# Softmax, prologue and weight conversion of a fused attention and MoE kernel rewritten: one exponential per row group, loads in another order, low words written into the sum's buffer

## The chip, the core and the metric

The kernel runs on one core of a Trainium2 chip. The core has five engines with a queue of instructions each, taken in order: TensorE (PE; its weight loads are shown apart as PEld), VectorE (DVE), ScalarE (ACT), GpSimd (POOL) and SyncE (SP, which issues most of the transfers here). Sixteen DMA engines move data between HBM and the on-chip buffer. The metric is the device time of one execution in microseconds, the median of several.

## The reference

Three stages, one after the other, on 4608 tokens of 512 features:

```python
# attention inside chunks of 64 tokens, 8 batches x 8 heads x 576 x 64
scores = scale * (q_c @ k_c.transpose(...))          # scale = 1/sqrt(64)
scores = scores - scores.max(-1)
attn = exp(scores); attn = attn / (attn.sum(-1) + 1e-9)
x = attn @ v_c                                        # -> (4608, 512)
# a dense layer pair, 512 -> 2048 -> 512
h = x @ w_in
x = (h * sigmoid(1.702 * h)) @ w_out
# routed layer pair: 8 experts, one per token, 512 -> 1024 -> 512
do = (x @ w_skip) > 0; e = argmax(x @ w_gate); p = softmax(x @ w_gate)[e]
out[do] = x + p * (relu(x @ w1[e]) @ w2[e]); out[~do] = x
```

The weights `w_in` and `w_out` come as 64-bit floating-point numbers.

## The kernel before, in words

Each matrix product of the dense and the routed layers is made of three in a 32-bit matmul type: an operand is split into a high half (a cast by ScalarE) and a low half (the rest, by VectorE), and high x high, high x low and low x high are summed. The dense layers run in nine blocks of 512 tokens. In a block TensorE goes over 16 slices of 128 of the inner dimension: `emit_h` (12 matmuls of 512 columns, L296) fills `hps`, then `sg` (tanh on ScalarE, L299; a product on VectorE, L300), `gh` (ScalarE, L306) and `gl` (VectorE, L307) follow, and `emit_y` (12 matmuls, L316, L317, L320) adds to `yps`. The y of a slice is written one slice behind its h. After the blocks the routed layers run.

**Attention.** The four tiles of 128 tokens that block 0 needs are worked in a prologue (`A[0]` to `A[3]`); the other 32 (`St`) are worked inside blocks 0 to 7, five in block 0 and four in each later one, at slices given by a table, two tiles' matmuls at a time (`burst`). A tile has these steps: loads of q, k and v; `a`, transposes of q and k by TensorE and copies by ScalarE; `b`, scores, the row maximum (L166) and the subtraction of it (L168) by VectorE, the exponential by ScalarE (L173); `c0`, sum, addition, reciprocal and product by VectorE (L176 to L179); `c1`, transposes; `d`, the product with v and its copies to `x1` (L212). `split_x1` makes the high and low halves `xh` (L285, ScalarE) and `xl` (L286, VectorE) of the block's activations.

**Conversion of the weights.** `w_in` and `w_out` are 32 halves of 128x512 numbers of 64 bits, 512 KB each (`Half`; half 2i is `w_in`'s slice i, half 2i+1 is `w_out`'s). `load` brings one into one of three `raw` buffers. `s0`, two ScalarE steps: `r`, the high words with the exponent moved (L255, "the r-step" below), and `lf`, the low words scaled (L256), into a single buffer. `s1`: VectorE shifts `r` (L262, the shift) and joins the sign (L263, the or-step) into `a`, which has two buffers; POOL adds `lf` (L264). `s3`: ScalarE casts `a` to `whi` (L276), VectorE takes the rest as `wlo` (L277). A `tick` does one such step for several halves in turn and issues the load of the half three further on. Slice i of block 0 needs halves 2i and 2i+1; in all later blocks the converted weights stay.

**What sets the order.** The text calls `tick` once per step of the prologue from its second step on, and twice per slice of block 0. The text's order is not the engines' order: the program is built with a scheduler that reorders each engine's queue by its own times. What counts is therefore the built order. Buffers that two uses share tie them: the three `raw` buffers (a load waits until the half three before has been read by ScalarE and VectorE), the four `x2` buffers for `r`, and PSUM's two banks with the tag `at` for the scores.

## Time and profile before

| | us |
|---|---|
| median of 3 runs | 1224.9 (1224.62 to 1226.09) |
| the profiled execution, its own time | 1227.84 |
| its span, first to last instruction | 1226.1 |
| TensorE busy | 1182.7 (96%) |
| TensorE weight loads busy | 991.8 (81%) |
| VectorE busy | 783.9 (64%) |
| ScalarE busy | 490.2 (40%) |
| POOL busy | 144.6 (12%) |
| first `xh` / first `xl` / first matmul of block 0 | 47.25 / 48.34 / 48.73 |
| first store of block 0's result | 166.58 |
| the same store of blocks 1, 2 and 3 | 265.93, 364.98, 464.02 |

Times are counted from the start of the span. A row of a list of groups gives the line of the kernel, the engine, the operation, output and inputs, the shape, the count, then busy time and the mean of one, then the idle time of the engine just before these instructions and what ended it. A row of the timeline gives start, duration, engine, line and operation, and in brackets the idle time just before with its releaser. Matmuls overlap each other, so their durations add up to more than the time they take.

### The profile page before, as it was taken

The numbers are of one execution on the slowest core, as the hardware profiler recorded it, in microseconds if no ns is written. First come the engines' busy times: TensorE is split into PE (matmuls) and PEld (weight loads), VectorE is DVE, ScalarE is ACT, GpSimd is POOL, SyncE is SP. The second block draws the span as 40 slices with busy tenths as digits, with TensorE's granted clock in tenths as the row PEclk, the third lists the DMA queues.
The fourth block names the chain that finished last, engine by engine and source line by source line (L and its number), as shares of the span: only waits on it lengthen the run. The fifth ranks groups of instructions, "written<-read, shape, count | busy, mean of one in ns | idle before, by whom it ended". The sixth has DMA issues, their size and how long they took to land. (4 is left out here: it accounts for less than half of the span.)

```text
span 1226.1 us, 20893 instructions
## 1 busy us (share of the span) xinstructions
PE 1182.7 (96%) x7984; PEld 991.8 (81%) x7984; DVE 783.9 (64%) x1771; ACT 490.2 (40%) x825; POOL 144.6 (12%) x137
## 2 busy tenths in 40 slices
PE   6798999999999999999999999999999999999995
PEld 4576788888888888888888888888788989999885
DVE  5889578369349548647736935943985686665531
ACT  5867443343332333324334333332344454444320
POOL 2344000010010010000001001001021023231110
PEclk9999999999999999999999999999999999999998
DMA  9756331131122113113113113202344677666540
GB/s 211 208 175 178 112 102 27 44 104 26 27 68 78 28 31 107 32 31 95 35 36 104 26 28 92 55 10 69 130 139 131 215 170 265 215 228 227 195 144 8
DMA packets 181848, 129.00 MB, mean 105 GB/s; under 512 B 122336, under 2 KB 155360, under 8 KB 181617
## 3 DMA queue, kind: packets, MB, share of 16 engines
q1 hardware_dynamic: 177072, 117.09, 33.4%
q0 software_dynamic: 4672, 10.54, 2.5%
q8 instruction: 64, 1.05, 0.4%
q14 instruction: 40, 0.32, 0.1%
HBM read 103.59 MB, written 25.04 MB: 105 GB/s over the span
## 5 line engine op out<-in xcount | busy, mean ns | idle before, releaser
L316 PE MATMUL yps<-whi,gh 128*128 128x512 f32 x576 | 228.7, 397 | 6.4 <-ACT gh L306 6.4
L296 PE MATMUL hps<-xh,whi 128*128 128x512 f32 x576 | 231.6, 405 | 3.2 <-DVE sg L300 3.2
L296 PE MATMUL hps<-xl,whi 128*128 128x512 f32 x576 | 227.5, 395 | 0.0
L296 PE MATMUL hps<-xh,wlo 128*128 128x512 f32 x576 | 227.0, 394 | 0.0
L317 PE MATMUL yps<-wlo,gh 128*128 128x512 f32 x576 | 225.6, 392 | 0.0
L300 DVE SCALAR_TENSOR_TENSOR sg<-sg,hps 128x512 f32<-128x512 f32 x144 | 98.3, 684 | 172.1 <-ACT sg L299 171.1
L353 DVE CUSTOM_DVE_ANT_0 junk<-x,wg 128x512 f32<-128x512 f32 x256 | 175.8, 687 | 4.0
L543 DVE TENSOR_TENSOR elo<-rawe,ehi 128x1024 fp32r<-128x1024 f32 x88 | 107.6, 1224 | 84.6 <-ACT ehi L542 84.5
L320 PE MATMUL yps<-whi,gl 128*128 128x512 f32 x576 | 156.0, 393 | 0.0
L299 ACT ACTIVATE sg<-hps 128x512 f32<-128x512 f32 x144 | 85.8, 598 | 163.4 <-PE hps L296 163.2
L542 ACT CAST ehi<-rawe 128x1024 fp32r<-128x1024 f32 x88 | 92.3, 1049 | 139.6 <-PE h2p L608 69.4
L306 ACT ACTIVATE gh<-sg 128x512 fp32r<-128x512 f32 x144 | 91.0, 632 | 118.3 <-DVE sg L300 104.8
L316 PEld LDWEIGHTS yps<-whi,gh 128*128 128x128 f32 x576 | 108.3, 188 | 30.9 <-ACT gh L306 7.8
L296 PEld LDWEIGHTS hps<-xh,whi 128*128 128x128 f32 x576 | 108.5, 190 | 26.3 <-DVE sg L300 4.1
L296 PEld LDWEIGHTS hps<-xh,wlo 128*128 128x128 f32 x576 | 108.9, 189 | 22.6
L320 PEld LDWEIGHTS yps<-whi,gl 128*128 128x128 f32 x576 | 108.0, 189 | 22.6 <-DVE gl L307 0.3
L317 PEld LDWEIGHTS yps<-wlo,gh 128*128 128x128 f32 x576 | 108.5, 188 | 21.8
L296 PEld LDWEIGHTS hps<-xl,whi 128*128 128x128 f32 x576 | 109.2, 190 | 20.6
L307 DVE SCALAR_TENSOR_TENSOR gl<-sg,gh 128x512 fp32r<-128x512 f32 x144 | 99.0, 688 | 33.4 <-ACT gh L306 21.7
L406 POOL DMA_INDIRECT tab<-pr,pos x36 | 37.8, 1049 | 682.3 <-DVE st L166 335.0
L608 PE MATMUL h2p<-xT,ehi 128*128 128x256 f32 x640 | 117.2, 283 | 0.0
L608 PEld LDWEIGHTS h2p<-xT,ehi 128*128 128x128 f32 x640 | 101.9, 191 | 2.6
(172 smaller groups left out, 1520.5 us busy)
## 6 DMA issues: line engine op xcount, KB each, us to landing
rawe<-in_moe_w_dram SPq DMA_DIRECT2D x88, 512.0 KB, 4.0
v<-in_v_dram SPq DMA_DIRECT2D x144, 64.0 KB, 2.7
x2d<-x SPq DMA_DIRECT2D x36, 256.0 KB, 3.1
out_dram<-x SPq DMA_DIRECT2D x36, 256.0 KB, 3.8
q<-in_q_dram SPq DMA_DIRECT2D x32, 256.0 KB, 3.7
k<-in_k_dram SPq DMA_DIRECT2D x32, 256.0 KB, 3.7
raw<-in_moe_w_in_dram SPq DMA_DIRECT2D x16, 512.0 KB, 4.0
raw<-in_moe_w_out_dram SPq DMA_DIRECT2D x16, 512.0 KB, 3.3
```

The costliest lines, as they stand in the source:

```text
L296: PE.matmul(ps, a, b[:, kk], start=(n == 0), stop=(n == 3 * KD - 1))
L299: ACT.activation(out=sg, in_=ps, func=AF.Tanh, scale=0.851)
L300: DVE.scalar_tensor_tensor(sg, sg, 1.0, ps, op0=ALU.add, op1=ALU.mult)
L306: ACT.activation(out=gh, in_=sg, func=AF.Copy, scale=0.5)
L307: DVE.scalar_tensor_tensor(gl, sg, 0.5, gh.bitcast(F32), op0=ALU.mult, op1=ALU.subtract)
L316: PE.matmul(ys[t], gh[:, cs], wh, start=first, stop=False)
L317: PE.matmul(ys[t], gh[:, cs], wl, start=False, stop=False)
L320: PE.matmul(ys[t], gl[:, cs], wh, start=False, stop=last)
L353: DVE.tensor_tensor_reduce(junk, xs[t], wg[:, e, :] if e < NE else ws, 1.0, 0.0, ALU.mult, ALU.add, lg[:, t, e:e + 1])
L542: ACT.copy(out=hi, in_=raw)
L543: DVE.tensor_tensor(lo, raw, hi.bitcast(F32), op=ALU.subtract)
L608: PE.matmul(ps[:, f], a[:, c], self.xT[:, b, kk], start=(m == 0), stop=(m == 3 * KD - 1))
```

## The change

Three things are changed.

The softmax: the row maximum goes to `nm`, which is multiplied by minus the scale; the subtraction, the exponential and the row sum are then made by ScalarE in eight instructions of 128x64 per tile, which read the scores from PSUM, with `nm` as a bias column and the sum written out to `st`. VectorE's subtractions and its sum fall away.

The prologue: all q, k and v are loaded ahead of halves 1 and 2, half 0 after the second tile; `tick` begins at the fifth step instead of the second; `split_x1` stands ahead of the last tick of the prologue.

The conversion: the low words are written into the buffer `a` itself, VectorE's or-step works in place on `r`, and POOL adds `r` to `a`. `a` has three buffers: two as before and one in the space that `lf` had.

```diff
         def b_post(self, ps):
             self.p = self.T[0].rearrange("p j (g k) -> p j g k", g=2)
-            pw = self.p.rearrange("p (x h) g k -> p h g x k", h=2)
             self.st = ap.tile([P, NHP, 2], F32, tag="st", name="st", bufs=2)
+            sc = float(D) ** -0.5
+            nm = ap.tile([P, 2, NHP], F32, tag="nm", name="nm", bufs=2)
             for h2 in range(2):
-                DVE.tensor_reduce(self.st[:, :, h2], ps[h2], axis=AX.X, op=ALU.max)
-            for h2 in range(2):
-                DVE.tensor_tensor(
-                    pw[:, h2], ps[h2].rearrange("p (g x) k -> p g x k", g=2),
-                    self.st[:, :, h2:h2 + 1].rearrange("p (g x) o -> p g x o", g=2).to_broadcast(
-                        [P, 2, 2, CH]), op=ALU.subtract,
-                )
-            ACT.activation(out=self.p, in_=self.p, func=AF.Exp, scale=float(D) ** -0.5)
+                DVE.tensor_reduce(nm[:, h2], ps[h2], axis=AX.X, op=ALU.max)
+            DVE.tensor_scalar(nm, nm, -sc, None, op0=ALU.mult)
+            for hp in range(NHP):
+                for h2 in range(2):
+                    g, j = divmod(2 * hp + h2, NHP)
+                    ACT.activation(out=self.p[:, j, g], in_=ps[h2][:, hp], func=AF.Exp, scale=sc,
+                                   bias=nm[:, h2, hp:hp + 1], accum_out=self.st[:, j, g:g + 1])
 
         def c0(self):
-            DVE.tensor_reduce(self.st, self.p, axis=AX.X, op=ALU.add)
             DVE.tensor_scalar(self.st, self.st, 1e-9, None, op0=ALU.add)
...
-            self.lf = mp.tile([P, HW], F32, tag="junk", name="lf")
+            m = 2 * self.i + self.half
+            if m % 3 < 2:
+                self.a = fp.tile([P, HW], F32, tag="a", name="a", bufs=2)
+            else:
+                self.a = mp.tile([P, HW], F32, tag="junk", name="a")
             ACT.activation(out=self.r, in_=hwf, func=AF.Abs, scale=2.0 ** -112)
-            ACT.activation(out=self.lf.bitcast(U32), in_=bits[:, :, 0], func=AF.Copy, scale=2.0 ** -29)
+            ACT.activation(out=self.a.bitcast(U32), in_=bits[:, :, 0], func=AF.Copy, scale=2.0 ** -29)
 
         def s1(self):
-            self.a = fp.tile([P, HW], F32, tag="a", name="a", bufs=2)
             ru, au = self.r.bitcast(U32), self.a.bitcast(U32)
             DVE.tensor_scalar(ru, ru, 3, None, op0=ALU.logical_shift_left)
-            DVE.scalar_tensor_tensor(au, self.hw, 0x80000000, ru, op0=ALU.bitwise_and, op1=ALU.bitwise_or)
-            POOL.tensor_tensor(au, au, self.lf.bitcast(U32), op=ALU.add)
+            DVE.scalar_tensor_tensor(ru, self.hw, 0x80000000, ru, op0=ALU.bitwise_and, op1=ALU.bitwise_or)
+            POOL.tensor_tensor(au, ru, au, op=ALU.add)
...
-    A[0].load_qk()
-    A[0].load_v()
-    halves[0].load()
-    A[1].load_qk()
+    for t in range(TPB):
+        A[t].load_qk()
+        A[t].load_v()
+        if t == 1:
+            halves[0].load()
     halves[1].load()
-    A[1].load_v()
-    A[2].load_qk()
     halves[2].load()
-    A[2].load_v()
-    A[3].load_qk()
-    A[3].load_v()
...
             A[tau - 3].d()
-        if tau >= 1:
+        if tau == TPB + 2:
+            xh, xl = split_x1(x1)
+        if tau >= TPB:
             tick()
...
-    xh, xl = split_x1(x1)
```

The built order shows what this does to the queues. The changed kernel's line numbers differ by a few from the old ones: its exponential is L172, the r-step L259, the low words L260, the shift L264, the or-step L265. Numbers behind a name tell buffers' uses apart.

On SP, the first loads after those of tile 0, before:

```order
L240 DMA raw64_110<-in_moe_w_in_dram 128x4x128
L122 DMA q_112<-in_q_dram 128x8x64
L122 DMA k_113<-in_k_dram 128x8x64
L245 DMA raw64_116<-in_moe_w_out_dram 128x512
L131 DMA v_118<-in_v_dram 64x4x64 x4
L122 DMA q_123<-in_q_dram 128x8x64
L122 DMA k_124<-in_k_dram 128x8x64
L240 DMA raw64_127<-in_moe_w_in_dram 128x4x128
L131 DMA v_129<-in_v_dram 64x4x64 x4
```

and after:

```order
L122 DMA q_110<-in_q_dram 128x8x64
L122 DMA k_111<-in_k_dram 128x8x64
L131 DMA v_114<-in_v_dram 64x4x64 x4
L239 DMA raw64_119<-in_moe_w_in_dram 128x4x128
L122 DMA q_121<-in_q_dram 128x8x64
L122 DMA k_122<-in_k_dram 128x8x64
L131 DMA v_125<-in_v_dram 64x4x64 x4
L122 DMA q_130<-in_q_dram 128x8x64
L122 DMA k_131<-in_k_dram 128x8x64
L131 DMA v_134<-in_v_dram 64x4x64 x4
L244 DMA raw64_139<-in_moe_w_out_dram 128x512
```

Half 0 stands behind tile 1, and halves 1 and 2 (`raw64_139` and the next) behind tile 3.

On ScalarE, the end of the prologue up to the first `xh`, from the cast ahead of half 8's r-step (`raw_488`), before:

```order
L276 CAST whi<-a 128x512
L255 ACTIVATE r<-raw_488 128x512
L256 ACTIVATE lf<-raw_488 128x512
L212 COPY x_100<-pv_457 128x2x128
L285 CAST xh<-x_99 128x512 x2
```

and after, from half 8's r-step (`raw_584`) on, where `sv` are the scores of the first `St` tile:

```order
L259 ACTIVATE r<-raw_584 128x512
L211 COPY x_100<-pv_408 128x2x128
L276 CAST whi<-a 128x512
L260 ACTIVATE a<-raw_584 128x512
L172 ACTIVATE qT,st<-sv_602,nm 128x64
L172 ACTIVATE qT,st<-sv_603,nm 128x64
L211 COPY x_99<-pv_440 128x2x128
```

Six more such exponentials and the copy of `pv_441` follow there before `L285 CAST xh<-x_99`; before, that tile's exponential stood behind `xh`. In both orders eight casts to `whi` and nine r-steps stand ahead of the first `xh`.

On VectorE in block 0, from the sixth `gl` to the seventh, before:

```order
L307 SCALAR_TENSOR_TENSOR gl<-sg,gh 128x512
L178 RECIPROCAL st<-st 128x8
L277 TENSOR_TENSOR wlo<-a,whi 128x512
L262 TENSOR_SCALAR r<-r 128x512
L179 TENSOR_TENSOR qT<-qT,st 128x512
L263 SCALAR_TENSOR_TENSOR a<-raw_1084,r 128x512
L277 TENSOR_TENSOR wlo<-a,whi 128x512
L300 SCALAR_TENSOR_TENSOR sg<-sg,hps 128x512
L263 SCALAR_TENSOR_TENSOR a<-raw_1162,r 128x512
L262 TENSOR_SCALAR r<-r 128x512
L307 SCALAR_TENSOR_TENSOR gl<-sg,gh 128x512
```

and after:

```order
L307 SCALAR_TENSOR_TENSOR gl<-sg,gh 128x512
L264 TENSOR_SCALAR r<-r 128x512
L277 TENSOR_TENSOR wlo<-a,whi 128x512
L265 SCALAR_TENSOR_TENSOR r<-raw_1314,r 128x512
L277 TENSOR_TENSOR wlo<-a,whi 128x512
L300 SCALAR_TENSOR_TENSOR sg<-sg,hps 128x512
L307 SCALAR_TENSOR_TENSOR gl<-sg,gh 128x512
```

Fewer steps of the attention stand between conversion and `gl`, and more of the conversion lies ahead of the seventh `gl`: 18 `wlo` between the first `xl` and it, where before it was the ninth `gl` that had 20 ahead of it.

## Rows read from the trace of the kernel before

**Rows 1.** Stretches: time, busy time of each engine (instructions), granted clock, DMA share, GB/s.
```profile
0.00:48.34 48.34, 29.56 (x350) 23.36 (x351) 30.60 (x65) 29.23 (x56) 13.11 (x21) 1.00 0.95 220
48.34:123.66 75.32, 67.01 (x396) 51.93 (x394) 69.79 (x108) 55.60 (x102) 34.61 (x22) 0.98 0.61 175
...
364.95:464.00 99.05, 99.05 (x694) 81.53 (x693) 62.61 (x167) 34.30 (x64) 4.14 (x5) 1.00 0.21 54
```
**Rows 2.** Waits of TensorE from 48.7 to 126: total, times, longest.
```profile
PE yps L316 <- ACT gh L306: 6.4, 5, 3.0
```
**Rows 3.** Timeline of the prologue: start, duration, engine, line, operation, idle before.
```profile
4.30 1.09 PE L141 MATMUL qTp<-ident,q 128*128 128x128 f32 x4 [4.30 <-DMA q<-in_q_dram]
...
35.75 0.67 ACT L255 ACTIVATE r<-raw 128x512 f32<-128x512 f32 x1 [0.55 <-DMA raw<-in_moe_w_out_dram]
...
41.67 0.67 ACT L255 ACTIVATE r<-raw 128x512 f32<-128x512 f32 x1 [1.04 <-DMA raw<-in_moe_w_out_dram]
...
45.88 0.67 ACT L255 ACTIVATE r<-raw 128x512 f32<-128x512 f32 x1
...
47.00 0.36 ACT L212 COPY x<-pv 128x256 f32<-128x256 f32 x1
47.25 1.15 ACT L285 CAST xh<-x 128x512 fp32r<-128x512 f32 x2
...
48.34 2.38 DVE L286 TENSOR_TENSOR xl<-x,xh 128x512 fp32r<-128x512 f32 x2
```
**Rows 4.** VectorE by group from 48.34 to 117.4: busy, mean of one, idle before.
```profile
L277 DVE TENSOR_TENSOR wlo<-a,whi 128x512 fp32r<-128x512 f32 x20 | 24.1, 1205 | 3.0 <-ACT whi L276 2.9
L263 DVE SCALAR_TENSOR_TENSOR a<-raw,r 128x512 uint32<-128x512 uint32 x22 | 16.0, 728 | 0.1
L262 DVE TENSOR_SCALAR r<-r 128x512 uint32<-128x512 uint32 x21 | 10.6, 504 | 1.6 <-ACT r L255 1.6
L307 DVE SCALAR_TENSOR_TENSOR gl<-sg,gh 128x512 fp32r<-128x512 f32 x9 | 6.1, 679 | 0.0
L300 DVE SCALAR_TENSOR_TENSOR sg<-sg,hps 128x512 f32<-128x512 f32 x9 | 6.0, 675 | 0.0
L286 DVE TENSOR_TENSOR xl<-x,xh 128x512 fp32r<-128x512 f32 x4 | 3.7, 954 | 0.0
```
**Rows 5.** Timeline of VectorE about the ninth `gl`.
```profile
116.75 0.68 DVE L307 SCALAR_TENSOR_TENSOR gl<-sg,gh 128x512 fp32r<-128x512 f32 x1
117.35 0.68 DVE L263 SCALAR_TENSOR_TENSOR a<-raw,r 128x512 uint32<-128x512 uint32 x1
```
**Rows 6.** Timeline of TensorE: ninth y, a burst, the end of block 0.
```profile
117.48 1.20 PE L320 MATMUL yps<-whi,gl 128*128 128x512 f32 x4
...
150.50 0.69 PE L207 MATMUL sv<-qT,v 64*64 64x64 f32 x32
...
151.59 0.50 PE L316 MATMUL yps<-whi,gh 128*128 128x512 f32 x1
...
163.73 0.39 PE L316 MATMUL yps<-whi,gh 128*128 128x512 f32 x1
...
165.54 1.07 PE L320 MATMUL yps<-whi,gl 128*128 128x512 f32 x4
```
**Rows 7.** ScalarE and VectorE by group, whole span.
```profile
L212 ACT COPY x<-sv 128x256 f32<-128x256 f32 x64 | 23.2, 365 | 107.7 <-DVE qT L168 106.0 <-PE sv L207 1.8
...
L173 ACT ACTIVATE qT<-qT 128x512 f32<-128x512 f32 x32 | 20.2, 633 | 0.0
...
L370 ACT ACTIVATE ex<-dl 128x32 f32<-128x32 f32 x9 | 2.1, 229 | 8.9 <-DVE dl L369 8.9
...
L353 DVE DVE_READ_ACCUMULATOR2_ANT lg<- 128x1 f32 x288 | 23.4, 81 | 0.0
```
**Rows 8.** Timeline of block 3 behind a burst: a `gh` and the y that uses it.
```profile
375.84 0.63 ACT L306 ACTIVATE gh<-sg 128x512 fp32r<-128x512 f32 x1 [1.67 <-DVE sg L300]
...
379.76 0.39 PE L316 MATMUL yps<-whi,gh 128*128 128x512 f32 x1
```

More of the change, by code (lines that the diff above doesn't have):

```diff
@@ L700, in tick @@
             halves[m].s1()
-        if 1 <= m <= 2 * NF:
-            halves[m - 1].s2()
         if m + 1 < 2 * NF:
```

2 lines of the change are left out of this document (removed).

## The prediction

> **What bounds the kernel now.** I read the profile's forty slices first, then the busy time by stage. In a steady block of 512 tokens TensorE is busy 99.05 of 99.05 us [rows 1]: nothing that the change does there can help, it can only harm. What can be gained lies ahead: the prologue (48.34 us until the first low half `xl` of the activations, in which TensorE works 29.6 us) and the first block, whose last matmul ends at 165.54 + 4 x 0.226 = 166.45 [rows 6]. From `xl` that is 118.1 us, against some 102 for a steady block with one burst more (99.05 plus 1.1 for the burst's matmuls [rows 6] and its transposes). TensorE's own wait in that block is small, 6.4 us in five pieces [rows 2]; the rest is spread over half-clock stretches and short gaps behind them. What it waits for is `gh`, and `gh` waits for VectorE: from `xl` to 123.66 VectorE is busy 69.8 of 75.3 us [rows 1], ScalarE 55.6.
>
> The prologue is paced by loads. ScalarE takes its queue in order, and the r-step of a weight half stands ahead of the attention's copies; at 35.75 and 41.67 it stood waiting for a load [rows 3]. Counting every load in the order of SP's queue fits one line: 3.05 us (the first q tile, 256 KB, at 4.30 [rows 3]) plus the bytes at 220 GB/s [rows 1]. For half 7 the queue holds 3072 KB of q, k, v, 342 of the table, 768 for the next attention tile and eight halves of 512 KB: 8278 KB, 38.5 us, so 41.6; the row says 41.67.
>
> **The change, part by part.** *Loads.* q, k, v of all four tiles now pass ahead of halves 1 and 2. The last v lands at 3.05 + 3584 KB / 220 GB/s = 19.7 us, some 5 us sooner. But up to half 8 the sum of bytes is the same in both queues, 9302 KB, which gives 46.4; in the trace its r-step ran at 45.88 without a wait [rows 3].
>
> *Fewer conversion steps ahead.* The program text moves three ticks behind the attention, but a scheduler sets the engines' order, and it pulls the conversions forward again: on ScalarE eight casts and nine r-steps stand ahead of the first `xh` before, and eight and nine after. So `xh` cannot run before half 8 is there. Before, the r-step, its low words and one copy are left at that point: 45.88 to 47.25 is 1.37 us [rows 3]. After, fourteen instructions are left: r-step, cast and low words at 0.56 each (two take 1.12 in [rows 3]), three copies at 0.25, and the eight exponentials of the fifth attention tile, which before stood behind `xh`.
>
> *The softmax.* One exponential of 128x512 (633 ns) becomes eight of 128x64, with a bias column and a sum. No such row exists. From below: behind a 128x256 copy the next instruction starts after 0.25 [rows 3]; 633 less 365 ns is 268 ns for 256 columns [rows 7], so 192 columns fewer leave 0.25 - 0.20 = 0.05 each. From above: the 32-wide exponential takes 229 ns, and where VectorE sums along the way the trace has a row of its own for the sum, 81 ns [rows 7], so 0.31. I take 0.31, since the 32-wide row is nearest in width and kind; a tile then costs ScalarE 2.5 us in place of 0.6. The tail comes to 3 x 0.56 + 3 x 0.25 + 8 x 0.31 = 4.9 us, `xh` to 45.88 + 4.9 = 50.8, and `xl`, 1.1 behind it [rows 3], to **51.9, 3.6 later**. With 0.05 each and half 8 at 45.7 it is 49.6; with 0.40 and half 8 at 46.4 it is 53.1.
>
> By the Trainium skill, "ScalarE: Activation LUTs", section "What ACT_TABLE_LOAD costs", an activation with a pointer bias takes 280 ns + 0.833 ns per element, and neighbours overlap by 93 ns: an estimate of 0.24 for 64 columns, by which the tail is 4.4 and the end of the sum 0.6 us earlier. It speaks against the split, since a fixed cost is paid eight times. No run here shows an activation with a bias column.
>
> On VectorE a tile loses two subtractions and a sum over 512 columns and gains one small multiply: about 1.3 us less.
>
> *VectorE in the first block.* The binding place moves. Before, it is the chain up to the ninth and tenth `gl`; after, the scheduler puts 18 halves ahead of the seventh. In the order, from the first `xl` to the seventh `gl`, stand 18 each of `wlo`, the or-step and the shift, 7 `sg`, 7 `gl`, 4 `xl` and eight small softmax steps. By the means of [rows 4] that is 21.7 + 13.1 + 9.1 + 4.7 + 4.8 + 3.8 + 2.0 = 59.2 us; neighbours overlap (117.35 follows 116.75 by 0.60, with a duration of 0.68 [rows 5]), so 0.08 for each of 78: 53.0 net. Before, VectorE stood still 4.6 us in that stretch, 3.0 for the cast behind POOL's sum and 1.6 for the r-step [rows 4].
>
> *Three buffers.* The low words go where the sum will stand, so their step no longer waits for POOL's previous sum; it waits for `wlo` of three halves before. Behind that wait ScalarE now holds `sg` and `gh` too. I take half of the 4.6 as kept, 2.3, with 0 and 4.6 as ends. The seventh `gl` is then done at 51.9 + 53.0 + 2.3 = 107.2.
>
> *What TensorE has left from there.* Before, from the third part of the ninth y (117.48) to the end: 49.0 us with 178 matmuls of 512 columns [rows 6]. After, from the third part of the seventh: 226, so 48 x 0.226 = 10.9 more (eight matmuls take 1.81 from 163.73 to 165.54), and nearly one burst, 1.09 from 150.50 to 151.59 [rows 6], of which five in 32 matmuls are done by then: 0.9. From these 60.8 us I take 0.9 off for late waits of TensorE, which lie in the old stretch as a few tenths each: 59.9. The block ends at **107.2 + 59.9 = 167.1, 0.7 us later than before**.
>
> *Steady blocks and the end: nothing.* There each burst costs ScalarE 1.9 us more. The `gh` behind a burst is done at 375.84 + 0.63 = 376.5 and its matmul starts at 379.76 [rows 8]: 3.3 us hide it. If that cover were gone, each microsecond past it would count 28 times.
>
> **The sum**: 0.7 us on the profiled execution (span 1226.1, its own time 1227.84, 2.9 above the median of the three runs); the same difference on the median gives 1224.9 + 0.7 = **1225.6**.
>
> **The rivals.** *Faster.* VectorE's queue really is relieved: the third buffer removes all standing (0 in place of 2.3) and the exponentials are cheap (`xl` at 49.6): 49.6 + 53.0 + 59.9 = 162.5, 3.9 less: 1221.0. For it: both waits that it removes are in [rows 4]. Against it: VectorE was busy 93% anyway, and it starts later. *Slower, by POOL and VectorE.* `wlo` takes 1205 ns where a step of the same size, `gl`, takes 679 [rows 4]; I put that down to POOL's sums running beside it. The 18 halves stand closer together now. If `wlo`'s mean goes to 1.4, that is 18 x 0.2 = 3.6, and with standing of 4.6: 51.9 + 53.0 + 3.6 + 4.6 + 59.9 = 173.0, 6.6 more: 1231.5. It decides from about 2.5 us over my sum. *Slower, in the bursts.* If an exponential costs 0.31 + (3.3 - 1.9) / 8 = 0.49 or more, `gh` comes late in every burst; at 0.3 us each, 28 x 0.3 = 8.4: 1234. *The prologue really gets shorter* (attention alone sets its end): excluded, as the queue holds half 8 ahead of `xh`.
>
> **How the numbers follow.** A measurement of this kernel tells 0.2%, 2.4 us, from no change. The forecast, within 2.4 us, gets 0.43; its own range is 1222.5 to 1227.4. Faster gets 0.22, slower by POOL and VectorE 0.23, slower in the bursts 0.12. So faster 0.22, same 0.43, slower 0.35. The range that leaves out a tenth on each side reaches to the faster case at 1221.0 and a little beyond, and takes in the slower one at 1231.5: 1220 to 1233.
>
> **What would show it.** ScalarE's exponentials at 0.3 us start to start; the ninth r-step (half 8) near 46 and the first `xl` near 52; VectorE without gaps until the seventh `gl` near 107; the first x2d store near 167; steady blocks 99.05 long. I am wrong if `xl` comes before 49, if VectorE shows gaps of several us in the first block, or if TensorE waits for `gh` in a steady block.

## The result: slower by 17 us, half of it in blocks called safe

| | before | after | difference |
|---|---|---|---|
| median, us | 1224.8 | 1242.1 | ratio 1.0144 (95%: 1.0126 to 1.0161) |
| profiled execution: own time / span, us | 1227.84 / 1226.1 | 1242.57 / 1240.8 | 14.7 of span |
| first `xl` | 48.34 | 52.73 | +4.4 |
| first store to `x2d` of block 0 | 166.58 | 172.45 | +5.9 |
| the same of block 2 | 364.98 | 374.36 | +9.4 |
| of block 6 | 761.16 | 773.75 | +12.6 |
| of block 8, the last | 947.58 | 960.79 | +13.2 |
| end of the span | 1226.1 | 1240.8 | +14.7 |

The forecast was no change, 1225.6, with a range to 1233. The medians lie 17.3 us apart and the two profiled executions 14.7, because the one profiled before took 3.0 us more than its median. The marks in the table say where the loss sits: 4.4 us ahead of `xl`, 1.5 from there to the first store of block 0, 7.3 in the blocks behind it, 1.5 in the last stage. Half of it is in the blocks that the prediction had set at nothing.

The stretches of the changed kernel, which answer to [rows 1] (time; busy time of TensorE, its weight loads, VectorE, ScalarE, GpSimd; granted clock; DMA share; GB/s):

```profile
0.00:52.73 52.73, 29.70 (x351) 23.71 (x352) 28.31 (x59) 38.73 (x132) 13.88 (x22) 0.80 0.83 210
52.73:123.66 70.93, 60.85 (x373) 47.75 (x372) 62.70 (x91) 55.10 (x123) 29.16 (x18) 0.93 0.53 158
...
374.36:474.21 99.85, 99.85 (x694) 81.25 (x693) 58.73 (x159) 40.88 (x124) 4.08 (x5) 1.00 0.20 54
```

The last line is a steady block: 99.85 us for 99.05, TensorE busy in all of it at full clock, and the same 694 records as before. TensorE waits for nobody there and still needs 0.8 us more for the same matmuls. ScalarE's 6.6 us more in that block are no wait of TensorE. In the first line ScalarE has 38.73 us of work in place of 29.23, and the granted clock is 0.80 in the mean (parts of the stretch at full speed, parts at half) where it was 1.00; one kernel below (e7) has the same prologue with 1.00 and `xl` at the same time, so the clock did not set that mark. In the second line it is 0.93 where it was 0.98; in e7 it is 0.98 there, and block 0 ends 0.5 us sooner.

The end of the prologue on ScalarE and the first `xl`, to set beside [rows 3] (start, duration, engine, line, operation, idle before):

```profile
46.63 0.67 ACT L259 ACTIVATE r<-raw 128x512 f32<-128x512 f32 x1 [0.33 <-DMA raw<-in_moe_w_in_dram]
...
48.78 0.31 ACT L172 ACTIVATE qT<-sv,nm 128x64 f32<-128x64 f32 x1
48.98 0.20 ACT L172 ACTIVATION_READ_ACCUMULATOR qT<-sv,nm 128x1 f32 x1
49.07 0.32 ACT L172 ACTIVATE qT<-sv,nm 128x64 f32<-128x64 f32 x1
...
51.62 1.22 ACT L285 CAST xh<-x 128x512 fp32r<-128x512 f32 x2
```
```profile
52.73 1.29 DVE L286 TENSOR_TENSOR xl<-x,xh 128x512 fp32r<-128x512 f32 x2
```

Half 8's r-step, then 4.99 us of queue, then `xh`. From one exp to the next it is 0.29 us.

VectorE from `xl` to the end of the seventh `gl`, against [rows 4] (busy, mean ns, idle before), and TensorE's waits from 52.7 to 130, against [rows 2] (total, times, longest):

```profile
L265 DVE SCALAR_TENSOR_TENSOR r<-raw,r 128x512 uint32<-128x512 uint32 x18 | 15.7, 872 | 0.2
L264 DVE TENSOR_SCALAR r<-r 128x512 uint32<-128x512 uint32 x18 | 14.1, 783 | 0.0
L277 DVE TENSOR_TENSOR wlo<-a,whi 128x512 fp32r<-128x512 f32 x19 | 13.9, 738 | 0.0
L307 DVE SCALAR_TENSOR_TENSOR gl<-sg,gh 128x512 fp32r<-128x512 f32 x7 | 7.0, 994 | 0.7 <-ACT gh L306 0.7
...
L178 DVE TENSOR_TENSOR qT<-qT,st 128x512 f32<-128x512 f32 x2 | 2.2, 1099 | 0.1
```
```profile
PE hps L296 <- DVE sg L300: 6.6, 3, 4.5
...
PE yps L316 <- ACT gh L306: 0.8, 1, 0.8
```

The standing of VectorE behind casts and r-steps that [rows 4] show is gone; that much of the change works. What TensorE waits for has changed too: mostly VectorE's `sg`, which frees the accumulator of the next `hps`, and hardly ScalarE's `gh`.

The last exp of block 3's first burst, the `gh` behind it and the first matmul that uses this `gh`, which answer to [rows 8]:

```profile
384.28 0.35 ACT L172 ACTIVATE qT<-sv,nm 128x64 f32<-128x64 f32 x1
...
386.50 0.63 ACT L306 ACTIVATE gh<-sg 128x512 fp32r<-128x512 f32 x1 [0.76 <-DVE sg L300]
```
```profile
391.14 0.39 PE L316 MATMUL yps<-whi,gh 128*128 128x512 f32 x1
```

It is done at 387.13, its matmul starts at 391.14: 4.0 us of cover. The smallest cover among the sixteen `gh` of this block is 1.7 us, and from 374 to 773 us the trace lists no wait of TensorE. The rival that wanted `gh` late in the bursts is out.

### The profile page after: what moved, and what is told of

It reads as the page before. It is cut to its first block, busy times and chain, and to the rows that moved or that the text cites. A ratio compares the mean times of both kernels' runs of the same rounds, so it can differ in the third digit from the quotient of the medians.

```text
span 1240.8 us, 21325 instructions
## 1 busy us (share of the span) xinstructions
PE 1189.6 (96%) x7984; PEld 992.7 (80%) x7984; DVE 753.9 (61%) x1699; ACT 551.3 (44%) x1365; POOL 146.6 (12%) x137
## 5 line engine op out<-in xcount | busy, mean ns | idle before, releaser
L300 DVE SCALAR_TENSOR_TENSOR sg<-sg,hps 128x512 f32<-128x512 f32 x144 | 98.5, 685 | 170.7 <-ACT sg L299 170.6
L307 DVE SCALAR_TENSOR_TENSOR gl<-sg,gh 128x512 fp32r<-128x512 f32 x144 | 102.6, 713 | 50.3 <-ACT gh L306 48.7
L172 ACT ACTIVATE qT<-sv,nm 128x64 f32<-128x64 f32 x256 | 76.5, 325 | 110.8 <-DVE nm L168 110.8
```

Of the source, the lines that this page charges most:

```text
L300: DVE.scalar_tensor_tensor(sg, sg, 1.0, ps, op0=ALU.add, op1=ALU.mult)
L307: DVE.scalar_tensor_tensor(gl, sg, 0.5, gh.bitcast(F32), op0=ALU.mult, op1=ALU.subtract)
```

## The experiments

Eighteen kernels, in five batches, each timed beside the kernel before (e12 in a single run). `xl` and block 0 (its first store) are from the profiled execution; a steady block is the distance between the first stores of two blocks from block 3 on.

| kernel | median, us | ratio to before (95%) | `xl` | block 0 | steady block |
|---|---|---|---|---|---|
| before | 1224.8 | | 48.34 | 166.58 | 99.05 |
| after | 1242.1 | 1.0144 (1.0126 to 1.0161) | 52.73 | 172.45 | 99.85 |
| e1 softmax alone | 1241.3 | 1.0122 (1.0098 to 1.0146) | 55.05 | 173.01 | 99.85 |
| e2 prologue alone | 1227.6 | 1.0006 (0.9995 to 1.0017) | 42.87 | 165.17 | 99.04 |
| e3 buffers alone | 1230.2 | 1.0025 (1.0013 to 1.0037) | 48.97 | 168.88 | 99.05 |
| e4 all but softmax | 1226.6 | 1.0005 (0.9993 to 1.0017) | 43.82 | 164.52 | 99.05 |
| e5 new softmax in prologue | 1233.9 | 1.0043 (1.0028 to 1.0057) | 52.90 | 173.24 | 99.07 |
| e6 new softmax in bursts | 1243.5 | 1.0125 (1.0105 to 1.0145) | 46.34 | 173.40 | 99.85 |
| e7 after, whole groups | 1231.7 | 1.0029 (1.0018 to 1.0041) | 52.75 | 171.94 | 98.78 |
| e8 before, whole groups | 1225.7 | 0.9980 (0.9968 to 0.9991) | 47.58 | 164.42 | 98.81 |
| e9 after, bursts whole | 1236.3 | 1.0061 (1.0044 to 1.0077) | 53.02 | 173.07 | 98.47 |
| e10 after, `xh` first | 1247.8 | 1.0157 (1.0141 to 1.0172) | 44.69 | 179.25 | 99.85 |
| e11 old softmax, whole groups | 1225.2 | 0.9980 (0.9971 to 0.9989) | 44.38 | 165.04 | 98.81 |
| e12 no accumulator | 1243.5 | one run | 58.81 | 178.09 | 99.86 |
| e13 two exps | 1227.9 | 1.0001 (0.9989 to 1.0013) | 46.48 | 165.83 | 99.08 |
| e14 two exps, whole groups | 1226.2 | 0.9995 (0.9985 to 1.0005) | 47.18 | 167.03 | 98.76 |
| e15 ScalarE load, prologue | 1235.8 | 1.0072 (1.0053 to 1.0090) | 58.66 | 175.02 | 99.00 |
| e16 ScalarE load, all tiles | 1246.4 | 1.0161 (1.0143 to 1.0179) | 56.63 | 182.33 | 99.08 |
| e17 before, bursts whole | 1226.2 | 0.9992 (0.9982 to 1.0003) | 50.05 | 168.02 | 98.51 |
| e18 old softmax, bursts whole | 1225.2 | 0.9991 (0.9978 to 1.0003) | 44.60 | 164.79 | 98.51 |

The kernel before was timed again in each batch (1226.6 to 1228.0); the ratios use the runs of the same batch.

### The three parts taken apart

Three theories at first. A: the eight exps carry the loss. B: the low words' wait for `wlo`, with `sg` and `gh` queued behind it, carries it. C: block 0 starts with fewer converted halves. Each part of the diff goes alone on the kernel before.

Softmax alone:

```
-                DVE.tensor_tensor(
-                    pw[:, h2], ps[h2].rearrange("p (g x) k -> p g x k", g=2),
...
-            ACT.activation(out=self.p, in_=self.p, func=AF.Exp, scale=float(D) ** -0.5)
...
+                    ACT.activation(out=self.p[:, j, g], in_=ps[h2][:, hp], func=AF.Exp, scale=sc,
+                                   bias=nm[:, h2, hp:hp + 1], accum_out=self.st[:, j, g:g + 1])
...
-            DVE.tensor_reduce(self.st, self.p, axis=AX.X, op=ALU.add)
```

> The kernel before with the new softmax alone; nothing is left out. Theory A (the softmax's eight exponentials on ScalarE carry the loss, ahead of block 0 and in each burst): nearly the whole loss shows here, 1237 to 1243 us, first xl at 51 or later, steady blocks 99.6 or longer. Theory B (the low words' step behind a wait for wlo carries it): 1225 to 1229. Theory C (block 0 starts with fewer converted halves because of the prologue's order): 1225 to 1229.

Prologue alone (loads in the new order, ticks from `tau` 4 on):

```
...
-        if tau >= 1:
+        if tau == TPB + 2:
+            xh, xl = split_x1(x1)
+        if tau >= TPB:
             tick()
```

> The kernel before with the new prologue alone; nothing is left out. In its built order 5 casts stand ahead of the first xh, not 8. Theory A: no loss here; the attention alone leads xh, so xl comes at about 40 to 44 us instead of 48.3, and VectorE's queue in block 0 takes some of it back: 1219 to 1225. Theory B: 1222 to 1226. Theory C: the loss is here, 1232 to 1240, with VectorE busy without gaps to 115 us or later.

Buffers alone:

```
-            self.lf = mp.tile([P, HW], F32, tag="junk", name="lf")
+            if m % 3 < 2:
+                self.a = fp.tile([P, HW], F32, tag="a", name="a", bufs=2)
+            else:
+                self.a = mp.tile([P, HW], F32, tag="junk", name="a")
...
```

> The kernel before with the low words in the sum's buffer alone; nothing is left out. Theory A: little, 1222 to 1226, ScalarE's waits for POOL (3.7 us for the cast, 1.1 for the low words in the prologue before) become waits for wlo. Theory B: the loss is here, 1232 to 1240, with ScalarE standing 5 us or more for wlo. Theory C: 1222 to 1226.

Prologue and buffers together, with the old softmax:

> The changed kernel with the old softmax; nothing is left out. Theory A: faster than before, 1217 to 1224, steady blocks at 99.05 again. Theory B and theory C: most of the loss stays, 1234 to 1242.

The softmax alone gives 1.0122 where the whole change gives 1.0144, so A holds for the loss. B would need e3 to lose most; it loses 3.2 us, 0.25%. That is more than A allowed: in its first 170 us ScalarE's casts wait 14.6 us for GpSimd's sums where before they waited 3.7, and block 0 ends 2.3 us later. C would need e2 and e4 to lose; they come out level, though A had expected them to be faster than before. They show something else, too: the new prologue does bring `xl` forward by 5.5 us, and block 0 then takes 4 us longer from there (122.30 us against 118.24). With the new softmax this advance is not seen, because the scheduler fills the freed prologue again: 7 r-steps stand ahead of `xh` on ScalarE in e4, 9 in the changed kernel, 12 in e1.

### Where the softmax costs: tiles of the prologue, tiles of the bursts

One line chooses between the two softmaxes by the tile's number:

```
+        def b_post(self, ps):
+            (self.b_post_n if self.t < TPB else self.b_post_o)(ps)
```

> The changed kernel, with the old softmax in the 28 tiles of the bursts and the new one only in the four tiles of the prologue. Theory O (what the blocks lose is TensorE's order: in the built program a steady block of the changed kernel changes 40 times between 512-column matmuls and the narrow ones of the attention, one of before 34 times, and 0.8 us over 6 changes is 0.13 us for each): this kernel has 34 changes, so its steady blocks take 99.05 us; the prologue's loss stays, xl at 51 to 54 us and block 0 done at 171 to 173 us, and the whole is 5 to 7 us over before, 1230 to 1232 us. Theory R (the blocks lose by the exps themselves, which hold ScalarE in each burst) gives the same blocks here, since the exps are gone from them too; the run gives the share of the prologue. Theory A2 (the prologue's loss is the conversions that the scheduler has put ahead of xh in ScalarE's queue, 10 r-steps here): xl late as in the changed kernel. If the prologue's loss comes from elsewhere, xl is near 44.

The mirror image (new softmax where `self.t >= TPB`):

> The changed kernel, with the old softmax in the four tiles of the prologue and the new one in the 28 tiles of the bursts. 40 changes in a steady block, 7 r-steps ahead of xh in ScalarE's queue. Theory O and theory R: steady blocks 99.85 us (blocks 1 and 2 about 100.9), as in the changed kernel. Theory A2: xl at 43 to 45 us, block 0 done at 164 to 167 us, so the whole is that of before less 1 or 2, and 8.8 for blocks and tail: 1231 to 1234 us. If the prologue's loss were not its own softmax's, block 0 would end at 172 and the whole at 1240.

The steady blocks split cleanly: 99.07 us with the new softmax in the prologue alone, 99.85 with it in the bursts alone. Block 0 does not split: either half alone ends it at 173 us, and both together at 172. For e6 the expectation failed by 10 us for that reason: its `xl` is early, at 46.34, but TensorE then waits 14.7 us in block 0 in place of 9.6 in e4.

### The steady blocks: exps, or TensorE's order

The first burst of block 3 in the trace of the changed kernel, on TensorE (start, duration, line; the program's 32 narrow matmuls are 64 records):

```profile
375.13 0.39 PE L296 MATMUL hps<-xh,wlo 128*128 128x512 f32 x1
375.45 0.56 PE L206 MATMUL sv<-qT,v 64*64 64x64 f32 x18
375.94 0.50 PE L316 MATMUL yps<-whi,gh 128*128 128x512 f32 x1
376.27 0.39 PE L317 MATMUL yps<-wlo,gh 128*128 128x512 f32 x1
...
377.43 0.84 PE L320 MATMUL yps<-whi,gl 128*128 128x512 f32 x3
378.20 0.40 PE L206 MATMUL sv<-qT,v 64*64 64x64 f32 x11
...
378.93 0.39 PE L317 MATMUL yps<-wlo,gh 128*128 128x512 f32 x1
379.16 0.40 PE L320 MATMUL yps<-whi,gl 128*128 128x512 f32 x1
379.49 0.69 PE L158 MATMUL sv<-kT,qT 64*64 64x64 f32 x30
...
380.11 0.50 PE L296 MATMUL hps<-xh,whi 128*128 128x512 f32 x1
380.44 0.39 PE L296 MATMUL hps<-xl,whi 128*128 128x512 f32 x1
```

The burst is cut in three. Between two wide matmuls it is 0.225 us; at a cut it is 375.13 to 376.27 = 1.14 us, which less two wide ones is 0.69 for 18 records. The three cuts cost 0.69, 0.60 and 0.83: 2.12 us. Nothing in these rows is a wait. In the built order the four bursts of a steady block are 9 + 8 + 15, 32, 1 + 31 and 32 matmuls, seven pieces, where before has four pieces of 32. With the transposes, TensorE changes 40 times between wide and narrow work, and 34 times before. So, theory O: the order costs; theory R: the exps themselves do. The test keeps the exps and ties TensorE's order, each matmul behind the one before it in the program, with no wait added:

```
+    def kept(ins):
+        if tail[1]:                       # blocks 1 to 7
+            if tail[0] is not None:
+                tc.add_manual_dep(ins.ins, tail[0].name, NoSync)
+            tail[0] = ins.ins
...
-                PE.matmul(ps, a, b[:, kk], ...)
+                kept(PE.matmul(ps, a, b[:, kk], ...))        (and the seven other matmuls and transposes)
```

> The changed kernel with TensorE's order of blocks 1 to 7 kept as the code is written (each matmul tied behind the one before it, an order without a wait): 12 of hps, 12 of yps, then the attention's group of that half pair in one piece. All of the eight exps stay. 26 changes in a steady block for 40. Theory O: 14 x 0.13 us less a block, 98.0 us; over seven blocks about 13 us less, 1228 to 1231 us. Theory R: the exps still hold ScalarE, so the blocks stay at 99.85 us or grow, since TensorE can no longer pass a late group; 1240 to 1246 us.

The same on the kernel before:

> The kernel before with the same order of TensorE in blocks 1 to 7: 26 changes in a steady block for 34. Theory O: 8 x 0.13 us less a block, 98.0 us, the same as the changed kernel so ordered; over seven blocks about 7 us less, 1217 to 1219 us. Theory R, or a price that is not the changes': 99.05 us, 1225 us; slower if the fixed order makes TensorE wait.

Both come to the same steady block, 98.78 and 98.81 us: with the order fixed, the eight exps cost TensorE nothing. Theory R falls. But O as priced falls too: 26 changes should have given 98.0. (The marks shift in these kernels. Before, 16 to 18 `hps` matmuls of the next block stand ahead of a block's last `yps`, in a fixed block none, and at block 0's end 12. So block 0's store comes 1.4 us early there, block 1's 95.4 us behind it, and block 7's, 101.1 us behind block 6's, pays it back; it is no gain. The marks of e11, e14, e17 and e18 shift in the same way.)

The price is then read by kind, over two steady blocks of each trace, as the time from the last wide start ahead of a piece to the second wide start behind it, less the wide ones' 0.225 us. A piece of one transpose costs 0.13 us, of four 0.45, of eight 0.89: 0.11 each, and nothing for a cut. The 64-wide pieces cost 0.46 for 2 records, 0.60 for 16, 0.83 for 30, 1.30 for 62 or 64. A cut burst pays some 0.4 us for each piece beyond the first. This says that fixing the bursts alone is enough and even better, which a run with only their pieces tied tests:

```
+                tail[1] = 0 < j < NB - 1
                 burst(St[kb] if kb < NST else None, St[kb - 1] if kb else None)
+                tail[1] = False
+                after_burst[0] = 0 < j < NB - 1     (the next hps is tied behind the burst)
```

> The changed kernel with one thing tied in TensorE's order, in blocks 1 to 7: the 32 narrow matmuls of a burst (16 for the values, 16 for the scores) stay one piece, behind the matmuls written ahead of them, and the next hps begins behind them. Steady block: 4 such pieces for 7; the transposes stay as cut up as they were (34 changes for 40). In the traces an uncut burst costs 1.30 to 1.33 us of TensorE, one cut 2 + 62 records 1.76, one cut 16 + 18 + 30 2.14; transposes cost 0.11 us each, cut or not. Theory O2 (only the cuts in the 64-wide groups cost): 0.44 + 0.82 = 1.26 us less, a block of 98.6 us, below that of the kernel with all groups fixed (98.78), which has 26 changes. Theory O1 (each change costs the same): between 99.85 and 98.78 by the changes, 99.4 us. Theory R (the exps): 99.85. Whole: 1231 to 1234 us by O2, 1238 by O1.

98.47 us, below every kernel with all groups fixed, as only the price by pieces has it (98.6 expected; a price by changes 99.4). A burst of this kernel in the trace, with 0.32 us ahead of it and 0.34 behind:

```profile
378.26 0.39 PE L330 MATMUL yps<-whi,gl 128*128 128x512 f32 x1
378.58 0.69 PE L213 MATMUL sv<-qT,v 64*64 64x64 f32 x32
379.09 0.65 PE L165 MATMUL sv<-kT,qT 64*64 64x64 f32 x32
379.67 0.50 PE L303 MATMUL hps<-xh,whi 128*128 128x512 f32 x1
380.01 0.39 PE L303 MATMUL hps<-xl,whi 128*128 128x512 f32 x1
```

From 378.26 to 380.01 it is 1.75, less 0.45: 1.30 us, where the cut burst took 2.12. Before, one burst of the four runs values and scores mixed:

```profile
443.18 0.39 PE L320 MATMUL yps<-whi,gl 128*128 128x512 f32 x1
443.49 0.68 PE L207 MATMUL sv<-qT,v 64*64 64x64 f32 x16
...
445.43 0.39 PE L296 MATMUL hps<-xl,whi 128*128 128x512 f32 x1
```

From 443.18 to 445.43, less 0.45, it is 1.80 us (the 1.91 in an expectation further down is a misreading). Four bursts: 5.2 us a block in e9, 6.5 in the changed kernel, 5.7 before. The difference of 0.8 between the last two is what a steady block lost. With all groups fixed (e7, e8) one piece of four transposes takes 0.90 us for 0.45, in front of a `gh` for which TensorE waits 0.2; that is where they stay behind e9.

The whole kernel missed its expectation by 2 us. Block 1 took 102.2 us, and the last stage 283.2, the longest of all these kernels. Of the 3.7 us of block 1 above a steady block, 1.6 are a wait for `gh` and 1.1 a stop inside its fourth burst, which takes 2.36 us for 1.30; the rest stays open.

The Trainium skill, "TensorEngine Tiling (Array Packing)", section "Key Properties", says that changing the tiling mode drains TensorE. The runs agree: 64x64 pieces among 128x128 ones pay about 0.4 us each, transposes, which stay 128x128, pay nothing.

### Block 0: what ends it late

Theory A2: `xh` and `xl` wait for conversions that the scheduler has put ahead of them; tied behind `xh`, they no longer hold it up. Rival C: the conversions and exps have to be done anyway, and only come later.

```
+    def later(ins):
+        if behind[0]:                     # what the code writes behind split_x1 of the prologue
+            tc.add_manual_dep(ins.ins, last_xh[0].ins.name, NoSync)
...
-            ACT.activation(out=self.r, in_=hwf, func=AF.Abs, scale=2.0 ** -112)
+            later(ACT.activation(out=self.r, in_=hwf, func=AF.Abs, scale=2.0 ** -112))
...                                       (the low-word step likewise)
-            ACT.copy(out=hi, in_=self.a)
+            later(ACT.copy(out=hi, in_=self.a))
```

> The changed kernel with ScalarE's order tied in the prologue: r-steps, low-word steps and casts that the code writes behind xh stay behind its last copy, so 3 r-steps, 4 low-word steps and 2 casts stand ahead of xh for 9, 9 and 6. Theory A2 (block 0 ends late because xh and xl wait for conversions that the scheduler has put ahead): xl at 42 to 45 us for 52.73, block 0 done at 164 to 167 us for 172.45, the whole 1235 to 1237 us. Rival C (what ends block 0 late is work that has to be done anyway, ScalarE's 32 exps and VectorE's conversions; put behind xh it is only later): xl early, block 0 done at 171 to 174 us, TensorE waiting in block 0 for wlo, sg or gl about 8 us more than now; the whole 1240 to 1243 us. Blocks 3 to 6 at 99.85 us by both.

(Ahead of `xh` the changed kernel has eight casts, as the section on the change says, not six.) `xl` comes 8 us sooner, and block 0 ends 6.8 us later. A2 falls, and the result lies beyond what C expected. TensorE's longest waits in this block (total, times, longest), of 18.0 us in all where the changed kernel has 10.5:

```profile
PE hps L303 <- DVE sg L307: 6.1, 3, 2.2
PE hps L303 <- ACT whi L283: 4.3, 2, 3.1
PE yps L323 <- ACT gh L313: 2.8, 1, 2.8
```

Now ScalarE's cast to `whi` itself is late, 3.1 us of it at 162. An early `xl` alone is worth nothing; the halves must be converted by then.

How an exp is priced: without its accumulator output, the sums by VectorE.

```
                     ACT.activation(..., func=AF.Exp, scale=sc,
-                                   bias=nm[:, h2, hp:hp + 1], accum_out=self.st[:, j, g:g + 1])
+                                   bias=nm[:, h2, hp:hp + 1])
...
+            DVE.tensor_reduce(self.st, self.p, axis=AX.X, op=ALU.add)
```

> The changed kernel with the eight exps without accum_out, and the sums taken by VectorE from the written values, as before. For the price of an exp: from start to start it is 0.29 us with its accumulator row of 217 to 220 ns. If that row is what sets the distance, the exps follow each other at 0.10 to 0.20 us, and ScalarE's busy time falls from 551 us by 256 times the difference, 25 to 50 us; if it lies beside the exp, the distance stays at 0.29. TensorE's steady blocks: 99.85 us if the order stays cut as it is (40 changes in the built order here too).

```profile
51.53 1.75 ACT L172 ACTIVATE qT<-sv,nm 128x64 f32<-128x64 f32 x8 [0.49 <-DVE nm L168]
```

Eight in 1.75 us with a last one of 0.33: 0.20 us apart. The accumulator row costs 0.09 us of the 0.29. But the scheduler put 12 r-steps ahead of `xh` here, and `xl` came at 58.81: the time saved was filled.

Take the exps' time away, and keep the rest of the new softmax: one maximum for four heads, and two exps for a tile.

```
+            for h2 in range(2):
+                DVE.tensor_reduce(nm[:, h2:h2 + 1], ps[h2].rearrange("p h k -> p (h k)"), axis=AX.X, op=ALU.max)
+            DVE.tensor_scalar(nm, nm, -sc, None, op0=ALU.mult)
+            for h2 in range(2):
+                ACT.activation(out=pw[:, h2], in_=ps[h2].rearrange("p (g x) k -> p g x k", g=2), func=AF.Exp,
+                               scale=sc, bias=nm[:, h2:h2 + 1])
```

> New prologue and new buffers; the softmax takes its scores from the accumulator bank and its maximum as a bias column, as the changed kernel does, but with one maximum for the four heads of a bank, so two exps of 128x256 for a tile in place of eight of 128x64; the sums are taken by VectorE. VectorE still loses the two subtractions. 7 r-steps, 6 low-word steps and 5 casts stand ahead of xh, bursts are whole (34 changes in a steady block). Theory A3 (block 0 ends late since the eight exps take 2.3 us of ScalarE for a tile; what else the new softmax does is harmless): xl at 43 to 45 us, block 0 done at 163 to 166 us, blocks of 99.05 us, 1224 to 1227 us. Rival S (the new structure itself: scores held in their bank until the exps are through, the maximum on the way to them): xl near 50, block 0 done near 172, 1232 us or more.

Add that time to the old softmax, in the prologue's four tiles:

```
             ACT.activation(out=self.p, in_=self.p, func=AF.Exp, scale=float(D) ** -0.5)
+            if self.t < TPB:
+                for j in range(NHP):
+                    for g in range(2):
+                        ACT.activation(out=self.p[:, j, g], in_=self.p[:, j, g], func=AF.Identity, scale=1.0,
+                                       bias=zero, accum_out=js[:, j, g:g + 1])
```

> New prologue and buffers with the old softmax (xl 43.8 us, block 0 done at 164.5, 1226.6 us), and behind the exp of each of the four tiles of the prologue eight steps of 128x64 on ScalarE that leave the values as they are, with a bias column and an accumulator output: the time of the eight exps without their place in the softmax. 11 r-steps and 10 low-word steps stand ahead of xh in the built order for 7 and 6. Theory A3 (ScalarE's time in the prologue, and what the scheduler puts into the queue behind it, end block 0 late): xl at 52 to 56 us, block 0 done at 172 to 175, blocks of 99.05 us, 1234 to 1237 us. Rival S: xl at most 2.4 us later for each tile on the path, block 0 done at 166 to 168, 1229 us.

Both go to A3. With two exps block 0 ends at 165.83 and the whole at 1227.9, a microsecond above what was said (`xl`, at 46.48, is 1.5 us later than said); with eight idle steps on the old softmax block 0 ends at 175.02 (`xl` even later than said, 58.66) and the whole at 1235.8 of 1234 to 1237 expected. The exps of e13 against those of the changed kernel (busy, mean ns):

```profile
L171 ACT ACTIVATE qT<-sv,nm 128x256 f32<-128x256 f32 x64 | 26.8, 471 | 103.4 <-DVE nm L169 103.4
```
```profile
L172 ACT ACTIVATE qT<-sv,nm 128x64 f32<-128x64 f32 x256 | 76.5, 325 | 110.8 <-DVE nm L168 110.8
L172 ACT ACTIVATION_READ_ACCUMULATOR qT<-sv,nm 128x1 f32 x256 | 55.5, 217 | 0.0
```

So ScalarE's time for the eight exps, with what the scheduler makes of it, is enough to end block 0 late, and the new structure costs little (165.83 for 164.52 in e4). Time and order move together in e15, which has 11 r-steps ahead of `xh` for 7, and no run parts them. The number of steps ahead of `xh` alone does not do it: the kernel before has the changed kernel's nine r-steps and eight casts there and ends block 0 at 166.58. The load on all tiles:

> The same load behind the exp of all 32 tiles: ScalarE has 2.3 us more in every burst, more than in the changed kernel, but the built order keeps the bursts of the steady blocks whole (4 pieces, 26 changes). Theory O2: steady blocks of 98.5 to 98.8 us, no slower for the load. Theory R (the load itself costs each burst): 99.85 us or more. Blocks 0 and 1 have cut bursts (3 and 8 pieces more), so block 0 is done at 173 to 177 us and the whole is 1234 to 1240 us.

```profile
384.01:483.09 99.08, 99.08 (x694) 81.79 (x693) 62.45 (x167) 44.22 (x128) 4.58 (x5) 1.00 0.20 54
```

A steady block with 44.22 us of ScalarE's work, more than the changed kernel's 40.88, takes 99.08 us, with TensorE busy in all of it. It is not the 98.5 to 98.8 expected, as its four whole bursts cost 1.48 us in the mean and not 1.30 (two of them run values and scores mixed), but with more load than the changed kernel it stands level with before: theory R is out a second time. Block 0 and the whole miss what was said: 182.3 for 173 to 177, and 1246.4 for 1234 to 1240. Block 0 ends another 7.3 us later than in e15, with the load in its five bursts. That the two loads add up here and not in e5, e6 and the changed kernel (173, 173, 172) is not explained.

### Versions that might beat both

Old softmax, new prologue and buffers, whole groups:

> The new prologue and the new buffers with the old softmax (1226.6 us, block 0 done at 164.5 us), and TensorE's order of blocks 1 to 7 fixed as the code is written. The kernel before gained 0.25 us a block and some 2 us at the end of block 0 by that. If the two gains add: block 0's stores at 162 to 163 us, blocks of 98.8 us, 1221 to 1223 us, the fastest here. If block 0 is bound by VectorE's conversions: stores at 164 to 165, 1224 us.

Two exps, whole groups:

> The same, with TensorE's order of blocks 1 to 7 fixed as the code is written (26 changes). By A3, and by what that order gave the old softmax (1225.2 us with the new prologue and buffers): 1221 to 1225 us, block 0's stores at 162 to 165, blocks of 98.8 us. By rival S 1231 us or more.

Neither reached its number. Fixed groups give 0.24 to 0.3 us in each steady block, and block 0, at 165.0 and 167.0, is not sooner than without them.

The last two tie `hps`, `yps` and the bursts and leave the transposes free, on the kernel before and on e4:

```
-                kept(PE.transpose(ps[:, hp, :], ...))     (tied, as in e8)
+                PE.transpose(ps[:, hp, :], ...)           (free)
```

> The kernel before with hps, yps and the bursts of blocks 1 to 7 tied in the order in which the code is written, and the transposes free. Four whole bursts in each steady block, and 36 changes between wide and narrow work, two more than before. Price by pieces (O2): the burst that mixes values and scores (1.91 us before) comes to 1.30, transposes cost nothing for being cut: steady blocks of 98.4 to 98.6 us, the whole 1221 to 1224 us, 0.2 to 0.3% below before. Price by changes: 99.05 us or a little more, 1225 to 1228 us.

> The same order with the new prologue and buffers and the old softmax. By O2 steady blocks of 98.4 to 98.6 us and the whole 1222 to 1224 us; by the changes 99.05 and 1226 to 1228 us. If the prologue's gain is worth anything, it lies below e17; by e4 it does not.

The price by pieces holds on the kernel before too: 98.51 us in both, mean of blocks 3 to 6, though the built order changes 36 times for 34. The whole does not show it. e18 is 6.8 us ahead of before at block 8's store, but its last stage takes 280.8 us for 278.5, and the medians lie 0.1% below before with intervals that include 1. e8 and e11 lie 0.2% below with intervals that exclude 1; those intervals overlap with the ones of e17 and e18, so which of the four is fastest is not shown.

## Why the prediction was wrong, point by point

**First `xl`: right, 0.8 us short.** It said 51.9, and 52.73 was measured. Half 8's r-step came at 46.63 for 45.88 (0.33 of that a wait for its load), the tail behind it took 4.99 for 4.9, and an exp 0.29 for 0.31. The estimate of 0.24 that the prediction worked out from the Trainium skill, "ScalarE: Activation LUTs", section "What ACT_TABLE_LOAD costs", was too low for exps with an accumulator; without one they stand 0.20 apart. That the prologue would be filled again with conversions was also right; in e4, with seven r-steps ahead of `xh`, `xl` comes at 43.82.

**VectorE from `xl` to the seventh `gl`: 55.3 us said, 58.24 measured.** The conversions came out as added up, 43.9 us for 18 halves and 43.7 for these rows with one `wlo` more, but by luck: `wlo` took 13.9 us for 21.7, the or-step 15.7 for 13.1, the shift 14.1 for 9.1. (The steps that the prediction lists are 80, not 78, which changes its sum by 0.1.) The standing was over-priced, 1.0 for 2.3. What failed is the price of the other steps: seven `gl` at 994 ns for 679, and small softmax steps 4.6 us for 2.0. The rows show why. GpSimd's sums and VectorE's steps about them:

```profile
95.59 1.59 POOL L267 TENSOR_TENSOR a<-r,a 128x512 uint32<-128x512 uint32 x1 [0.72 <-ACT whi L276]
...
104.72 1.57 POOL L267 TENSOR_TENSOR a<-r,a 128x512 uint32<-128x512 uint32 x1 [0.72 <-DVE r L265]
108.55 1.57 POOL L267 TENSOR_TENSOR a<-r,a 128x512 uint32<-128x512 uint32 x1 [2.26 <-ACT a L260]
```
```profile
95.95 1.52 DVE L264 TENSOR_SCALAR r<-r 128x512 uint32<-128x512 uint32 x1
...
102.44 0.41 DVE L264 TENSOR_SCALAR r<-r 128x512 uint32<-128x512 uint32 x1
...
105.07 1.77 DVE L307 SCALAR_TENSOR_TENSOR gl<-sg,gh 128x512 fp32r<-128x512 f32 x1
...
108.90 0.68 DVE L300 SCALAR_TENSOR_TENSOR sg<-sg,hps 128x512 f32<-128x512 f32 x1
110.28 0.69 DVE L307 SCALAR_TENSOR_TENSOR gl<-sg,gh 128x512 fp32r<-128x512 f32 x1 [0.70 <-ACT gh L306]
```

The shift that starts inside GpSimd's sum takes 1.52 us, the one outside it 0.41; the `gl` at 105.07 takes 1.77 where its like at 110.28 takes 0.69. A sum stretches a VectorE step that starts inside it, but not every one: `sg`, which reads `hps` from PSUM, takes 0.68 at 108.90, and all four `sg` that start inside a sum in this stretch take 0.67 to 0.68. Before, the step that paid was mostly `wlo` (1205 ns in [rows 4]); now `wlo` takes 738, and the shifts, the or-steps, two small softmax steps and two of the seven `gl`, which TensorE waits for, pay. The means of [rows 4] held this toll in the wrong rows. The Trainium skill, "Advanced Engine Details and Errata", section "Miscellaneous Facts", says that GpSimd shares a read and a write interface with VectorE, and that this conflicts with VectorE instructions that have two inputs in SBUF (the on-chip buffer) or run in a 2-port mode. The trace agrees so far as `gl`, with two such inputs, is stretched and `sg`, with one, is not. The rival "slower by POOL and VectorE" had the same cause in mind, but both of its terms failed: `wlo` at 0.74 us for its 1.4 and standing of 1.0 for its 4.6. The loss came on other steps, 2.9 us in place of its 5.9.

**TensorE's remainder: 59.9 us said, 61.5 measured** (to the first store). From the end of the seventh `gl` TensorE was busy 60.9 of 61.5 us. The work had been counted well, 60.8; the 0.9 taken off it for late waits should have stayed, and a wait of 0.6 for a late `wlo` came on top. The three terms together, 0.8 + 2.9 + 1.6 = 5.3, are what block 0 ended behind the 167.1 forecast.

**Steady blocks: nothing said, 7.3 us measured.** This is the step that failed worst. The argument looked at one way to lose there, a late `gh`, found 3.3 us of cover and stopped. The cover held (4.0 us behind the same burst). But the change also let the scheduler move TensorE's own matmuls, and a burst cut in pieces costs 0.4 us for each further piece. The built order showed the pieces in advance; the prediction looked at ScalarE's and VectorE's order and took TensorE's for unchanged. Blocks 1 and 2 took 1.1 us more than the other blocks, and the rows put that in one place, the fourth burst of each, whole in the order. In block 1, with GpSimd beside it:

```profile
251.42 0.39 PE L320 MATMUL yps<-whi,gl 128*128 128x512 f32 x1
...
252.25 0.88 PE L158 MATMUL sv<-kT,qT 64*64 64x64 f32 x21
253.50 0.45 PE L158 MATMUL sv<-kT,qT 64*64 64x64 f32 x11 [0.38 <-issue]
...
254.22 0.39 PE L296 MATMUL hps<-xl,whi 128*128 128x512 f32 x1
```
```profile
252.25 1.14 POOL L406 DMA_INDIRECT tab<-pr,pos  x1 [95.11 <-DVE bs L396]
```

By the same measure that burst costs 2.35 us for 1.30. So cut bursts make some 5.2 of the 7.3 us (0.8 in each of blocks 2 to 6, 1.3 in block 7), and these two stops 2.1. Blocks 1 and 2 of e9 and e10 have the stop too, and in all six cases it begins 0.2 us after GpSimd starts an indirect DMA; that the one causes the other was not tested, so the cause of this part stays open.

**The last stage: +1.5 us.** Its code is the same. From block 8's store to the end it takes 278.5 us before, 280.0 after, and from 277.9 (e3) to 283.2 (e9) in the eighteen kernels, with no pattern that follows the edits. The forecast's zero for it cannot be called wrong by these runs.

**The range.** With TensorE's groups fixed the changed kernel takes 1231.7 us (e7), inside the range to 1233; with the bursts alone whole it takes 1236.3 (e9), outside. Up to block 8's store the two are level (951.8 and 952.3), and e9's last stage is 3.9 us longer in the profiled executions. What block 0 lost, 5.3 us on 1225.6, would have stayed inside by itself; what the later blocks lost carried the kernel beyond.

## What to carry to other kernels

Where an engine is busy all the time, a change elsewhere can still cost it time through its order: compare the built order of the bound engine first, and look for narrow matmuls that are split up among wide ones. An exp of 64 columns with a bias column and an accumulator costs 0.29 us, so splitting one of 512 columns into eight trades 0.6 us of ScalarE for 2.3; one maximum for the four heads of a bank keeps the subtraction inside the exp and needs two exps, with the sums on VectorE. (It rests on the heads' maxima lying near each other: a head far below the shared maximum would have exps near zero.) An early start of one operand is worth nothing while the others come from the same queues.

## What the runs showed of the hardware

A piece of 64x64 matmuls among 128x128 ones of 512 columns costs TensorE some 0.4 us once, whatever its length, on top of its own matmuls (0.46 us for 2 records, 1.30 for 64); transposes of 128x128 cost 0.11 us each and nothing for being split. ScalarE's accumulator output is a row of its own of 217 ns, of which 0.09 us shows in the distance from one exp to the next. A shift on VectorE takes 0.41 us alone and 1.52 when it starts inside GpSimd's sum; `sg`, which reads PSUM, takes 0.67 to 0.68 either way. The mean granted clock of the prologue was 0.80 in the changed kernel and 1.00 in e7, whose prologue is the same; `xl` came at 52.73 and 52.75.
